# Row maxima of an attention kernel turned by a VectorE transpose of 32 by 32 blocks, in place of a matmul with the identity

## The chip, the cores and the metric

The kernel runs on one core of a Trainium2 chip. The metric is the device time of one execution in microseconds (us), smaller is better. A profile of one execution shows what each engine did: TensorE (PE, and PEld for its weight loads), VectorE (DVE), ScalarE (ACT), GpSimd (POOL) and SyncE (SP), whose queue issues most DMAs.

## The reference

One block of attention with 32 heads of 16 dimensions over 2048 rows, gated by a two-layer MLP of the same normalized input. All data are float32.

```python
xn = _layernorm(x, axis=-1)                                # x: 1 x 2048 x 512
qkv = (xn @ wqkv) ...                                      # 32 heads of 16
scores = jnp.einsum("bhqd,bhkd->bhqk", q, k) * (Dh ** -0.5)
p = _softmax(scores, axis=-1)
o = jnp.einsum("bhqk,bhkd->bhqd", p, v)
s = o.transpose(0, 2, 1, 3).reshape(B, S, D) @ wo
h = _gelu(jnp.einsum("bsd,df->bsf", xn, w1) + b1)          # F = 1376
g = _silu(jnp.einsum("bsf,fd->bsd", h, w2) + b2)
return x + s * g
```

## The kernel before

**Units.** The attention is cut into 32 units `u`: 8 groups of 4 heads times 4 chunks of 512 query rows. Every unit is worked twice. A first pass (`s_mm`, L179, and `s_max`, L185) makes the scores with the query rows on the partitions, one tile of 128 queries by 512 keys per head, and VectorE reduces each tile to maxima (`mx`). The tiles live in a ring of PSUM banks (`s_tile`): two banks in the first stage, three in the second. The second pass (`t_one`, L722 and L724) makes the scores again, this time with the keys on the partitions; two more rows of the contraction carry the negative maximum of each query, so that TensorE subtracts it, and ScalarE takes the exponential (`slot<-pst`, `slot<-ps`). `pv_step` (L787) multiplies by the values, with four heads in four column strips of 32, 16 steps per unit.

**The end of a unit.** When the first pass of a unit is done, its maxima must go from "query on the partition" to "query along the free axis". `s_end0` (L235) reduces the maxima of the key chunks on VectorE and negates them (`nm`, L240, 128 partitions by 4 heads x 4 query tiles), and POOL splits them into a rounded high part and the rest (`nmh`, L243 and L244: 128 x 2 x 16). Some 8 or 12 ticks later `s_end1` (L257) multiplies `nmh`, as weights, with the identity of 128 x 128 on TensorE. The result, 32 rows (part, head, query tile) of 128 queries, stands in a PSUM bank taken from the score ring (first stage) or from the ring of the second pass (`t_tile`, four banks). `s_end2` (L262) copies it to SBUF (`mh`), with ScalarE in the first stage (L265) and VectorE in the second (L267), and SP writes it to a scratch in DRAM (`mh_d`, L268). Later `load_mh` (L150) reads it back as the two more rows of `qt`.

**Stages.** From 57 us TensorE works at the MLP and the remaining projections (`mm`, L573), with two row halves of 64 rows used side by side, and `fill` interleaves 576 tiles of first-pass scores at due row counts. `FILL0`, `ROWS` and `put` set the due rows: an end takes a place in this order and moves what follows by two rows. From 484 us each of 512 steps holds four tiles of the second pass, the `pv` of the step before and three quarters of a score tile pair, in the order `TXSTTSTYV`; after the `V` the ticks advance and `flush` may end a unit. In the last part, from 1515 us, the first pass is over, and the steps hold output projections (`w_mul`, L79) in its place. The instruction order of every engine is written out by the program (a manual schedule); no planner decides it.

Of the kernel before, what the change touches and what calls it, by code (L numbers as in the profile page):

```python
# [8 lines left out]
F32 = mybir.dt.float32  # L9
F32R = mybir.dt.float32r  # L10
AF = mybir.ActivationFunctionType
# [5 lines left out]
P = 128  # L17
# [7 lines left out]
NCH = S // CH  # L25
F = 1376
FT = (F + P - 1) // P
GH = 4
# [4 lines left out]
LEAD = 144  # L33
# [3 lines left out]
FILL0 = 38  # L37
# [10 lines left out]
def fused(ctx: ExitStack, tc: tile.TileContext, x, wqk, wv, wo, w1, b1, w2, b2, out):  # L48
    nc = tc.nc
# [15 lines left out]
    mh_d = dpool.tile([NG * NCH, 2, GH, CH], F32, name="mh_d")  # L65

    ident_r = keep.tile([P, P], F32R, name="ident_r")
# [13 lines left out]
            if then:  # L81
                then()

    QS, QT, MX, NM, MH = {}, {}, {}, {}, {}
    SYNC = mybir.DependencyInfo(mybir.DependencyClass.Sync, mybir.DependencyReason.DATA)
    qss = []
    NU = NG * NCH
# [3 lines left out]
    def s_tile(held=False):  # L91
        pool = s_ring.pop(0)
        if not held:
            s_ring.append(pool)
        return pool.tile([P, CH], F32, name="ps"), pool
# [57 lines left out]
    made = [0, 0]  # L153
    done = {u: 0 for u in range(NU)}
    later, ended, errands, sent = [], [], [], set()

    def tick():
        for e in later:
            e[0] -= 1

    def flush():
        while later and later[0][0] <= 0:
            u = later.pop(0)[1]
            run_off()
            s_end1(u)
            s_end2(u)

    def at_of(job):
        u, st, p = job
# [29 lines left out]
    def s_one(a):  # L199
        made[a] += 1  # L200
        s_whole(heads[made[a] - 1], a)
# [29 lines left out]
    def run_off():  # L231
        while put_off:
            put_off.pop(0)()
# [21 lines left out]
    prog = {}  # L255

    def s_end1(u):  # L257
        pm = s_tile()[0] if "seen" in prog else t_tile()
        nc.tensor.matmul(pm[:2 * GH * NCH, :P], NM.pop(u).rearrange("p i a -> p (i a)"), ident_r, start=True, stop=True)  # L259
        MH[u] = pm  # L260

    def s_end2(u):  # L262
        mh = qring.tile([2 * GH * NCH, P], F32, name="mh", bufs=1)
        if "seen" in prog:
            nc.scalar.activation(mh, MH.pop(u)[:2 * GH * NCH, :P], AF.Copy)  # L265
        else:
            nc.vector.tensor_copy(mh, MH.pop(u)[:2 * GH * NCH, :P])  # L267
        nc.sync.dma_start(mh_d[u].rearrange("i j (q s) -> (i j q) s", s=P), mh)  # L268
        sent.add(u)

    sa = ExitStack()
# [19 lines left out]
    VQ = 3  # L291
    first = [[("v", t // NCH, t % NCH) for t in range(i, i + 4)] for i in range(NT - 4 * VQ, NT, 4)]
    qs = [(2, 0), (2, 2)] + [(g, 0) for g in range(3, NG)] + [(g, 2) for g in range(3, NG)]
    nu, pairs = len(ms) // 2, []
# [8 lines left out]
    for j in range(len(pairs)):  # L303
        for h in range(2):
# [4 lines left out]
            due = next((i for i in range(j, len(pairs)) if is_m[i]), len(pairs))  # L309
# [212 lines left out]
    qring = ctx.enter_context(tc.tile_pool(name="qring", bufs=2, side="right"))  # L522
# [16 lines left out]

    prog.update(n=0, pe=0, seen=0)  # L540
    writer = {}
    s_when, put, row = [], [0], [0, 0]
    ndown = sum(1 for e in plan if e[0] == "down")
    ROWS = 12 * (4 * VQ + 2 * len(pairs)) + 6 * ndown - 10 + 2 * LEAD - 2 * (LEAD // 16 - 1) - FILL0

    def fill(a):
        due = FILL0 + put[0] + sum(made) * ROWS // (4 * LEAD)
        if sum(made) < 4 * LEAD and row[a] >= due and (made[0] <= made[1]) == (a == 0):
            taken()
            if later and later[0][0] <= 0:  # L550
                put[0] += 2
                u = later.pop(0)[1]
                s_end1(u)
                s_end2(u)
                return
            s_one(a)
            row[a] += 1
            tick()

    def taken():  # L560
        prog["pe"] += 1
        s_when.append(prog["pe"])
        if len(s_when) > 2:
            prog["seen"] = max(prog["seen"], s_when[-3])
# [32 lines left out]
    def run(ops, hooks={}):  # L597
        for n, two in enumerate(zip(*ops)):
            prog["n"] += 1
            for a in range(2):  # L600
                fill(a)
                mm(a, *two[a])
            for h in hooks.get(n, []):
                h()
# [102 lines left out]
    def t_tile():  # L707
        turns[0] += 1
        if turns[0] < 5:
            pool = (ps_m, ps_x, ps_a, ps_b)[turns[0] - 1]  # L710
        else:
            pool = ps_m if turns[0] % 4 == 1 else ps_t
        return pool.tile([P, CH], F32, name="pst" if pool is ps_t else "ps")
# [230 lines left out]
    for n in range(L + 1):  # L944
        ua, ka = divmod(n, 16)
        want = due(n) - due(n - 1)
        i = 0
        for op in ORDER[want] if n > 1 else ("TTTTV", "TTSTSVT")[n]:
            if op in "SXY":
                s_op(op)  # L950
            elif op == "V":
                if n:
                    pv_step(*divmod(n - 1, 16))
                for _ in range(4):
                    tick()
                flush()
            else:
                if EARLY <= 4 * n + i < 4 * L:
                    t_one(ua, ka, i % 2, 1 - i // 2)
                for f, args in todo.get((n, i), []):  # L960
                    f(*args)
                i += 1
# [56 lines left out]
```

## Time and profile before

| | |
|---|---|
| median of 3 runs | 1606.27 us (1606.13 to 1606.79) |
| span of the profiled execution | 1603.9 us |
| PE busy | 1593.1 us, 99% |
| DVE busy | 1383.5 us, 86% |
| ACT busy | 1260.5 us, 79% |
| POOL busy | 377.5 us, 24% |

The profiled execution's own time is not listed apart from its span; the median of the runs lies 2.4 us above the span. A row of a group reads: line, engine, operation, what is written `<-` what is read, the form (partitions x elements, for matmuls rows*columns), the count, then busy us and the mean ns of one, then the idle time of the engine before them. A row of the order of time reads: start, length, engine, line, operation, and in brackets the idle time before it and what ended it. Ends of matmuls are modelled, so for TensorE the distance from start to start is what counts.

### The profile page before, as it was taken

How to read it: one execution, taken by the hardware profiler on the slowest of the kernel's cores; microseconds unless marked ns; L12 is line 12 of the kernel's file. 1: busy time of each engine (PE TensorE's matmuls, PEld its weight loads, DVE VectorE, ACT ScalarE, POOL GpSimd, SP SyncE). 2: the span in 40 equal slices, each digit the busy share in tenths (PEclk: the TensorE clock that was granted, in tenths of full speed). 3: DMA queues.
4: the chain of work that ended last, by engine and by line, in shares of the span. 5: the costliest groups of instructions: out<-in, count | busy, mean ns of one | idle time of the engine just before them, and what ended most of it. 6: DMA issues, size and time to landing. Idle time of an engine off the chain costs nothing.

```text
span 1603.9 us, 32476 instructions
## 1 busy us (share of the span) xinstructions
PE 1593.1 (99%) x12146; PEld 915.7 (57%) x12146; DVE 1383.5 (86%) x2267; ACT 1260.5 (79%) x2524; POOL 377.5 (24%) x398
## 2 busy tenths in 40 slices
PE   8999999999999999999999999999999999999998
PEld 7899989999994444444444444444444444444445
DVE  7489888888989999999999999999999999999734
ACT  4333443434339999999999999999999999999984
POOL 4145565766640001011100200100010000000144
PEclk9999999999999999999999999999999999999999
DMA  6525343454322113111410411221141111110152
GB/s 204 149 59 151 116 136 97 148 145 126 114 89 70 40 30 70 29 36 42 79 32 27 68 42 29 59 42 29 30 70 30 30 29 37 34 29 22 58 200 91
DMA packets 76798, 116.93 MB, mean 73 GB/s; under 512 B 25156, under 2 KB 26436, under 8 KB 75464
## 3 DMA queue, kind: packets, MB, share of 16 engines
q1 hardware_dynamic: 73180, 102.42, 22.4%
q0 software_dynamic: 3264, 12.35, 3.9%
q8 instruction: 96, 1.57, 0.4%
q14 instruction: 62, 0.51, 0.1%
q10 hardware_dynamic: 196, 0.07, 0.0%
HBM read 84.35 MB, written 25.97 MB: 69 GB/s over the span
## 4 chain that ended last, share of the span: by engine, by line
PE 97%; DVE 1%; ACT 0%; DMA 0%; issue 0%; SPq 0%; DVEq 0%; ACTq 0%
PE pv L787 32%; PE ps L179 18%; PE pst L722 16%; PE ps L573 12%; PE pst L573 7%; PE ps L722 5%; PE ps L79 3%; PE pv L573 2%; PE pst L79 1%; DVE slot L74 0%; DMA xt<-in_x 0%; PE pst L259 0%; DVE st L407 0%; PE ps L259 0%; DVE xn L421 0%
## 5 line engine op out<-in xcount | busy, mean ns | idle before, releaser
L185 DVE TENSOR_REDUCE mx<-ps 128x2 f32<-128x512 f32 x2048 | 1299.4, 685 | 153.3 <-PE ps L179 84.9
L724 ACT ACTIVATE slot<-pst 128x512 f32<-128x512 f32 x1533 | 835.1, 612 | 14.2 <-PE pst L722 4.1
L787 PE MATMUL pv<-slot,vsb 128*32 128x512 f32 x4096 | 545.3, 605 | 0.0
L179 PE MATMUL ps<-kt,slot 48*128 48x512 f32 (+1 forms) x1364 | 393.1, 376 | 0.0
L722 PE MATMUL pst<-qt,kt 50*128 50x512 f32 x1149 | 378.1, 430 | 0.5 <-DVE gt L655 0.3
L722 PEld LDWEIGHTS pst<-qt,kt 50*128 50x128 f32 x1149 | 183.0, 184 | 249.6 <-ACT slot L724 246.2
L724 ACT ACTIVATE slot<-ps 128x512 f32<-128x512 f32 x515 | 314.8, 612 | 12.9 <-PE pst L722 8.2
L179 PEld LDWEIGHTS ps<-kt,slot 48*128 48x128 f32 x1364 | 211.3, 184 | 34.2 <-DVE mx L185 23.3
L573 PE MATMUL ps<-slot,w1h 64*128 64x512 f32 x1088 | 220.5, 394 | 0.0
L179 PE MATMUL ps<-kt,qz 48*128 48x512 f32 x512 | 214.9, 420 | 0.0
L179 PE MATMUL ps<-slot,slot 48*128 48x512 f32 (+1 forms) x598 | 172.6, 376 | 0.0
L722 PE MATMUL ps<-qt,kt 50*128 50x512 f32 x387 | 163.0, 423 | 0.0
L573 PEld LDWEIGHTS ps<-slot,w1h 64*128 64x128 f32 x1088 | 152.9, 185 | 6.8 <-ACT junk L587 0.8
L787 PEld LDWEIGHTS pv<-slot,vsb 128*32 128x32 f32 x4096 | 80.6, 108 | 119.8 <-issue 112.0
L573 PE MATMUL ps<-slot,w1l 64*128 64x512 f32 x544 | 143.0, 392 | 0.0
L367 POOL TENSOR_TENSOR hl<-hg,hh 128x512 fp32r<-128x512 f32 x76 | 96.8, 1296 | 131.7 <-ACT hh L366 95.0
L722 PE MATMUL pst<-qt,slot 50*128 50x512 f32 x384 | 119.8, 424 | 0.0
L587 ACT ACTIVATE junk<-ident_r 1x1 f32<-1x1 f32 x92 | 18.0, 196 | 126.4 <-PE pst L573 123.2
L722 PEld LDWEIGHTS ps<-qt,kt 50*128 50x128 f32 x387 | 71.1, 184 | 69.4 <-ACT slot L724 56.5
L179 PEld LDWEIGHTS ps<-kt,qz 48*128 48x128 f32 x512 | 93.7, 183 | 17.4 <-DVE mx L185 0.6
L243 POOL CAST nmh<-nm 128x16 fp32r<-128x16 f32 x32 | 6.3, 197 | 413.1 <-PE pst L722 209.1
L722 PEld LDWEIGHTS pst<-qt,slot 50*128 50x128 f32 x384 | 61.5, 184 | 71.9 <-ACT slot L724 71.6
(150 smaller groups left out, 1744.9 us busy)
## 6 DMA issues: line engine op xcount, KB each, us to landing
raw<-in_w SPq DMA_DIRECT2D x88, 256.0 KB
qk_h<-hh SPq DMA_DIRECT2D x32, 256.0 KB
qk_l<-hl SPq DMA_DIRECT2D x32, 256.0 KB
qt<-qk_h SPq DMA_DIRECT2D x128, 64.0 KB
slot<-qk_h SPq DMA_DIRECT2D x92, 64.0 KB
xt<-in_x SPq DMA_DIRECT2D x16, 256.0 KB
g_d<-gt POOLq DMA_DIRECT2D x16, 256.0 KB, 3.1
qt<-qk_l SPq DMA_DIRECT2D x64, 64.0 KB
```

Source lines behind the costliest of these rows:

```text
L79: nc.tensor.matmul(ps, lhs[a], rhs[b], start=first and n == 0, stop=last and n == 2)
L179: return nc.tensor.matmul(ps[:, c0:c0 + w], QS[u][r, p, qi * P:(qi + 1) * P], kts[u // NCH % KB][p][r, k0:k0 + w], start=True, stop=True).ins
L185: nc.vector.tensor_reduce(MX[u][:, 2 * p:2 * p + 2, qi, ki][:, heads, parts], ps.rearrange("p (n c) -> p n c", c=HC), axis=AX.X, op=OP.max)
L243: nc.gpsimd.tensor_copy(hl[:, 0], nm)
L367: nc.gpsimd.tensor_sub(hl, raw, hh.bitcast(F32))
L573: i = nc.tensor.matmul(ps, lhs[r], rhs[r], start=first, stop=last).ins
L587: i = nc.scalar.activation(junk[:, :1], ident_r[:1, :1].bitcast(F32), AF.Copy).ins
L722: nc.tensor.matmul(ps, kts[g % KB][p][r, k * P:(k + 1) * P], QT[u][r, p, :], start=True, stop=True)
L724: nc.scalar.activation(PT[u, k][:, 2 * p + a, :], ps, AF.Exp, scale=SCALE)
L787: nc.tensor.matmul(PV[u][32 * j:32 * j + 32, :], vsb[:, k, h:h + 32], PT[u, k][:, j, :], start=(k == 0), stop=(k == NT - 1))
```

## The change

The matmul with the identity and the copy out of PSUM go. One VectorE instruction transposes the 128 x 32 elements of `nmh` in blocks of 32 by 32 within SBUF. Partition 32 b + r of `mh` then holds, for row r of (part, head, query tile), the 32 queries of block b. The DMA to `mh_d` puts this in order: 128 pieces of 32 elements, and not 32 pieces of 128. As an end no longer takes a place on TensorE, `put` and its part in `ROWS` go too, and `fill` puts a score tile in the same place.

```diff
     def s_end1(u):
-        pm = s_tile()[0] if "seen" in prog else t_tile()
-        nc.tensor.matmul(pm[:2 * GH * NCH, :P], NM.pop(u).rearrange("p i a -> p (i a)"), ident_r, start=True, stop=True)
-        MH[u] = pm
-
-    def s_end2(u):
-        mh = qring.tile([2 * GH * NCH, P], F32, name="mh", bufs=1)
-        if "seen" in prog:
-            nc.scalar.activation(mh, MH.pop(u)[:2 * GH * NCH, :P], AF.Copy)
-        else:
-            nc.vector.tensor_copy(mh, MH.pop(u)[:2 * GH * NCH, :P])
-        nc.sync.dma_start(mh_d[u].rearrange("i j (q s) -> (i j q) s", s=P), mh)
+        mh = qring.tile([P, 2 * GH * NCH], F32, name="mh", bufs=1)
+        nc.vector.transpose(mh, NM.pop(u).rearrange("p i a -> p (i a)").bitcast(F32))
+        nc.sync.dma_start(mh_d[u].rearrange("i j (q b s) -> b (i j q) s", b=NCH, s=2 * GH * NCH), mh)
         sent.add(u)
...
-    ROWS = 12 * (4 * VQ + 2 * len(pairs)) + 6 * ndown - 10 + 2 * LEAD - 2 * (LEAD // 16 - 1) - FILL0
+    ROWS = 12 * (4 * VQ + 2 * len(pairs)) + 6 * ndown - 10 + 2 * LEAD - FILL0
...
-        due = FILL0 + put[0] + sum(made) * ROWS // (4 * LEAD)
+        due = FILL0 + sum(made) * ROWS // (4 * LEAD)
...
             if later and later[0][0] <= 0:
-                put[0] += 2
-                u = later.pop(0)[1]
-                s_end1(u)
-                s_end2(u)
-                return
+                s_end1(later.pop(0)[1])
             s_one(a)
```

More of the change, by code (lines that the diff above doesn't have):

```diff
@@ L82, in mm3 @@
                 then()
-    QS, QT, MX, NM, MH = {}, {}, {}, {}, {}
+    QS, QT, MX, NM = {}, {}, {}, {}
     SYNC = mybir.DependencyInfo(mybir.DependencyClass.Sync, mybir.DependencyReason.DATA)
@@ L541, in fused @@
     writer = {}
-    s_when, put, row = [], [0], [0, 0]
+    s_when, row = [], [0, 0]
     ndown = sum(1 for e in plan if e[0] == "down")
-    ROWS = 12 * (4 * VQ + 2 * len(pairs)) + 6 * ndown - 10 + 2 * LEAD - 2 * (LEAD // 16 - 1) - FILL0
+    ROWS = 12 * (4 * VQ + 2 * len(pairs)) + 6 * ndown - 10 + 2 * LEAD - FILL0
     def fill(a):
-        due = FILL0 + put[0] + sum(made) * ROWS // (4 * LEAD)
+        due = FILL0 + sum(made) * ROWS // (4 * LEAD)
         if sum(made) < 4 * LEAD and row[a] >= due and (made[0] <= made[1]) == (a == 0):
@@ L550, in fill @@
             if later and later[0][0] <= 0:
-                put[0] += 2
-                u = later.pop(0)[1]
-                s_end1(u)
-                s_end2(u)
-                return
+                s_end1(later.pop(0)[1])
             s_one(a)
```

## The prediction

> **What bounds the kernel now.** I read the stretches first, to see which engine sets the pace of each stage; then the chain of waits, for what a unit of work takes with and without the step that changes; then the order of time around that step; then the groups of VectorE and the DMA issues. Rows of the stretches give start:end, length, and then for PE, PEld, DVE, ACT and POOL the busy time and the instructions.
>
> ```profile
> 57.00:484.00 427.00, 426.59 (x3545) 386.18 (x3545) 375.46 (x591) 163.35 (x369) 239.23 (x211) 1.00 0.41 119
> 484.00:1515.00 1031.00, 1030.89 (x7876) 441.44 (x7868) 939.52 (x1549) 1013.31 (x1994) 77.34 (x128) 1.00 0.18 41
> ```
>
> In the first stage (57 to 484) TensorE is never idle and ScalarE has much room. In the second (484 to 1515) TensorE is never idle either, ScalarE is busy for 98% and VectorE for 91%: whatever takes TensorE's time there costs its own length, and VectorE and ScalarE have little room to give. The granted clock is 1.00.
>
> What an end of a unit costs in the second stage is read from the chain of waits (start, length, what). These rows are the first `pv` matmul group of the units 1 to 5, each 16 steps after the one before.
>
> ```profile
> 519.96 1.06 PE pv L787 x8
> 553.70 1.06 PE pv L787 x8
> 587.46 1.07 PE pv L787 x8
> 620.83 1.06 PE pv L787 x8
> 654.36 1.06 PE pv L787 x8
> ```
>
> The stretch 587.46 to 620.83 takes 33.37 us and holds no end (no L259 matmul). The one from 620.83 takes 33.53 and holds one, at 623.84 below. The one from 519.96 takes 33.74 and holds one at 535.6. So an end costs 0.16 or 0.37, and the question is how much of the 0.37 is the matmul. In order of time on TensorE, and then on VectorE around 535.6:
>
> ```profile
> 623.84 0.25 PE L259 MATMUL pst<-ident_r,nmh 128*32 128x128 f32 x1
> 624.01 0.50 PE L722 MATMUL ps<-qt,kt 50*128 50x512 f32 x1
> ```
> ```profile
> 532.52 0.28 DVE L240 TENSOR_REDUCE nm<-mx 128x16 f32<-128x128 f32 x1
> 532.71 1.28 DVE L185 TENSOR_REDUCE mx<-ps 128x2 f32<-128x512 f32 x2
> 533.91 0.24 DVE L815 RECIPROCAL dr<-dr 128x16 f32<-128x16 f32 x1
> 534.07 1.84 DVE L185 TENSOR_REDUCE mx<-ps 128x2 f32<-128x512 f32 x3
> 535.87 0.28 DVE L267 COPY mh<-pst 32x128 f32<-32x128 f32 x1
> 536.42 0.69 DVE L185 TENSOR_REDUCE mx<-ps 128x2 f32<-128x512 f32 x1 [0.27 <-PE ps L179]
> ```
> ```profile
> 534.04 0.18 PEld L179 LDWEIGHTS ps<-slot,slot 48*128 48x128 f32 x1 [0.27 <-DVE mx L185]
> ```
>
> The next matmul starts 0.17 after L259, which is the whole 0.16. In the stretch with 0.37 there are also L240 and a reciprocal on VectorE, 1.5 to 3 us before the end, and behind them the weight load at 534.04 waits 0.27 for a `mx`: two short VectorE operations among the maxima held a PSUM bank of the score ring too long. That remains 0.21, and it stays: L240 and L815 are not touched.
>
> **The change part by part.** *Matmuls, stage two.* The groups of VectorE (line, operation, form, count | busy us, mean ns) give the number of ends.
>
> ```profile
> L240 DVE TENSOR_REDUCE nm<-mx 128x16 f32<-128x128 f32 x32 | 8.8, 276 | 0.1
> L815 DVE RECIPROCAL dr<-dr 128x16 f32<-128x16 f32 x32 | 7.8, 242 | 2.1 <-DMA dr<-os 2.1
> L267 DVE COPY mh<-pst 32x128 f32<-32x128 f32 x18 | 5.0, 276 | 0.1
> L267 DVE COPY mh<-ps 32x128 f32<-32x128 f32 x6 | 1.7, 277 | 0.1
> L848 DVE SCALAR_TENSOR_TENSOR slot<-slot,slot 128x512 f32<-128x512 f32 x4 | 7.3, 1825 | 0.4
> ```
>
> 32 ends, of which VectorE copies 24, so the other 8, copied by ScalarE, are in stage one. One of the 24 is in the tail (below). 23 x 0.16 = 3.7 us.
>
> *Matmuls, stage one.* Around an end there, on TensorE:
>
> ```profile
> 255.44 0.50 PE L573 MATMUL pst<-w2h,hh 64*128 64x512 f32 x2
> 255.88 0.25 PE L259 MATMUL ps<-ident_r,nmh 128*32 128x128 f32 x1
> 256.05 0.50 PE L573 MATMUL pst<-w2l,hh 64*128 64x512 f32 x2
> 256.39 0.40 PE L573 MATMUL pst<-w2h,hl 64*128 64x512 f32 x2
> 256.62 0.39 PE L179 MATMUL ps<-kt,qz 48*128 48x512 f32 x1
> 256.63 0.39 PE L573 MATMUL pst<-w2h,hh 64*128 64x512 f32 x1
> 256.86 0.39 PE L573 MATMUL pv<-w2h,hh 64*128 64x512 f32 x1
> 256.86 0.39 PE L573 MATMUL pst<-w2l,hh 64*128 64x512 f32 x1
> 257.09 0.39 PE L573 MATMUL pv<-w2l,hh 64*128 64x512 f32 x1
> ```
>
> From 256.62 to 257.09 four matmuls start, two at a time in the two row halves: 0.1175 each. From 255.44 to 256.62 six of them and L259 take 1.18; six alone would take 0.705. So L259, which uses all rows and lets nothing run beside it, costs 0.475 here, and 8 x 0.475 = 3.8 us. The slot that it held in the interleaving goes back to the scores: the due rows lose their 2 per end and the total gains the same 16, so the 576 score tiles of this stage still end with it.
>
> *The tail.* Steps start here at the output projection, from the chain of waits:
>
> ```profile
> 1515.47 1.60 PE ps L79 x6
> 1518.07 0.18 PE pst L259
> 1519.11 1.59 PE ps L79 x6
> 1522.36 1.59 PE ps L79 x6
> ```
>
> The step with the last end takes 3.64, the next 3.25. Of the 0.39 only 0.18 is L259; the rest lies in score matmuls that wait for banks, one of which L259 had taken. Between 0.18 and 0.39 I take 0.3.
>
> *The copies.* 8 on ScalarE in stage one: it is busy for 163 of 427 us, so nothing. 24 on VectorE, 0.276 each, give their place to the transpose.
>
> *The transpose*, 32 of them, 128 partitions by 32 elements. No row shows this operation. Nearest are L815 with 16 elements per partition (0.242) and L240 with 128 (0.276); the far end is L848 at 1.83, SBUF to SBUF too but 512 elements and two inputs. I take 0.26, the middle of the near pair. In stage two that is the copy's length, at the copy's place in VectorE's order. The copy's cover was partly L259 itself: without it the next maximum could start 0.17 sooner than 536.42, at 536.25, while a transpose begun at 535.87 ends at 536.13. So nothing is lost up to about 0.38; if the cover were gone, the price is what L240 and L815 cost, 0.21 per end. Below nothing: a gain is excluded where VectorE is not what TensorE waits for, but where an end falls beside an L240, up to the full 0.37 may go. In stage one the transposes are 8 x 0.26 = 2.1 us more for an engine that is busy for 375 of 427 us; hidden. A page of the Trainium skill, "VectorE: DVE Perf Modes", section "The three transpose paths", gives 311 ns for 128x128 of 2-byte elements on VectorE; by that price the sum would be the same, since it is under the 0.38. No run here shows it yet.
>
> *The new wait.* The transpose waits for POOL's `nmh`, as L259 did. Behind it in VectorE's order stand the score maxima, for which TensorE's score matmuls wait. POOL's second `nmh` operation, in stage two and in stage one:
>
> ```profile
> 534.35 0.22 POOL L244 TENSOR_TENSOR nmh<-nm,nmh 128x16 fp32r<-128x16 f32 x1
> ```
> ```profile
> 248.97 0.22 POOL L244 TENSOR_TENSOR nmh<-nm,nmh 128x16 fp32r<-128x16 f32 x1
> ```
>
> It is done 1.3 us before VectorE gets to 535.87, and 6.7 us before 255.88. In the built order two POOL subtractions stand ahead of `nmh` at three ends of stage one where they stood behind; even several us fit. No wait.
>
> *The write of the maxima.* Still one DMA per unit, of the same 16 KB, but from 128 partitions with 128 bytes each and not from 32 with 512. SP's queue (start, time to issue):
>
> ```profile
> 1518.59 0.32 SPq L268 DMA_DIRECT2D mh_d<-mh  x1
> 1521.68 1.36 SPq L150 DMA_DIRECT2D qt<-mh_d  x2
> 1538.66 0.32 SPq L816 DMA_DIRECT2D den_d<-dr  x1
> 1541.54 2.45 SPq L819 DMA_DIRECT2D dn<-den_d  x4
> ```
>
> L150 follows its write by 3.1 us. L816 writes 64 bytes from each of 128 partitions, issues in the same 0.32, and its reader follows after 2.9. So 128-byte lines need no more time: 0. Behind L268 and L150 in SP's queue stand loads and stores of other units, which then move by nothing either. What it costs if the row misleads is a rival below.
>
> *The sum:* 3.8 + 3.7 + 0.3 = 7.8 us. The profiled span of 1603.9 becomes 1596.1. The median of the runs, 1606.27, lies 2.4 above the span; that stays, so 1598.5.
>
> **The rivals.** *The transpose stalls as L240 does.* Among back-to-back maxima it holds a bank and TensorE loses 0.21 per end where it saved 0.16: stage two 23 x -0.05 = -1.2, in all 3.8 + 0.3 - 1.2 = 2.9, so 1603.4. For it: VectorE at 91%, and the wait at 534.04. Against: at the end's place VectorE idles 0.27 before the next maximum.
>
> *The whole 0.37 goes.* If L259 and the bank that it takes also make the wait at 534.04 dear, each end of stage two gives 0.37: 23 x 0.37 = 8.5, with 3.8 and 0.39 in all 12.7, so 1593.6. For it: the 33.74. Against: the wait comes before the matmul, and 33.53 shows ends without it.
>
> *The late write.* For the last unit the write and the read of the maxima stand 4 steps (of 3.25) ahead of the matmul that needs them: from about 1518.6 to 1528.1. If the read, whose issue ends at 1523.0, takes the 2.9 us that the write of L816 took, it lands at 1525.9, 2.2 ahead. If small lines doubled the write's 3.1, the matmul would wait 0.9: 1599.4. Against: L816. The Trainium skill, "DMA: Bandwidth & Descriptors", section "Specifications", states that below 512 B a transfer is done as a read-modify-write; that speaks against this change and would be the mechanism. The trace does not bear it out, since 64-byte lines took 2.9 and 512-byte lines 3.1.
>
> *Slower: the transpose is long.* If it took the 1.83 of L848, VectorE would come 1.83 - 0.38 = 1.45 late at each end of stage two, and with three banks always in use TensorE would lose that: 23 x 1.45 = 33. Stage one would lose at most the 8 x 1.83 = 15. Against the gain of 7.8 and with half of the latter, 1606.3 + 33 + 7 - 8 = 1638. It decides from a transpose of about 0.38 + 7.8 / 31 = 0.63 us. For it: no row of this operation. Against: all rows of short operands.
>
> **How the numbers follow.** Forecast 0.63, own range 1596 to 1601 (0.05 either way per end, stage one 3.0 to 4.1); a stall like L240's 0.13; all of it 0.11; late write 0.05; long transpose 0.08. 0.2% of the time, about what a measurement of this kernel can tell from no change, is 3.2 us, so faster means below 1603.1. Faster: 0.63 + 0.11 + 0.05 and 0.02 of the stall; same: 0.11 of it; slower: 0.08. The range goes from 1594.0 to 1603.5 and leaves out the long transpose and the edge of the two others.
>
> **What would show it.** Right: no L259; stretches between the `pv` rows at 33.35 to 33.6, with a short one near 33.4 also where an end lies; the first stage 3.8 shorter; a transpose row near 0.26; no idle time of DVE ascribed to L244; L150 about 3 us behind L268. Wrong: a transpose of over 0.4; weight loads of L179 that wait longer in total for `mx`; stretches still at 33.7; a wait for `qt` after 1515.

## The result, and the profile after

The changed kernel takes 1596.14 us (median; 1595.38 to 1596.83), the kernel before, on the same chip, 1606.53 (1606.13 to 1608.83). The ratio is 0.9937, with a 95% interval of 0.9925 to 0.995. The span of the profiled execution went from 1603.9 to 1593.6 us.

The stretches of the changed kernel, in the same columns as before (start:end, length, then busy time and instructions of PE, PEld, DVE, ACT and POOL):

```profile
57.00:480.00 423.00, 422.54 (x3544) 384.45 (x3545) 378.27 (x603) 162.97 (x364) 240.33 (x214) 1.00 0.42 122
480.00:1505.00 1025.00, 1024.99 (x7836) 439.12 (x7828) 935.20 (x1545) 1011.17 (x1991) 76.66 (x126) 1.00 0.19 41
```

TensorE still fills both stages, so what left its order left the time. The groups of VectorE by form (count | busy, mean ns | idle time before them):

```profile
L239 DVE TENSOR_REDUCE nm<-mx 128x16 f32<-128x128 f32 x32 | 8.8, 276 | 0.0
L802 DVE RECIPROCAL dr<-dr 128x16 f32<-128x16 f32 x32 | 7.8, 243 | 2.2 <-DMA dr<-os 2.2
L258 DVE STREAM_TRANSPOSE mh<-nmh 128x32 f32<-128x32 f32 x32 | 6.5, 202 | 0.0
```

The transpose takes 0.202 us, and the idle time ahead of all 32 of them is 0.0: none waits for POOL.

The chain of waits (start, length, what): the second `pv` group of the units 0 to 5, and the last steps with output projections around the last end. (The rows of the prediction, too, show each unit's second `pv` group and not its first; the unit lengths read from them are the same to some hundredths.)

```profile
479.71 1.07 PE pv L774 x8
...
513.09 1.06 PE pv L774 x8
...
546.62 1.07 PE pv L774 x8
...
580.21 1.06 PE pv L774 x8
...
613.60 1.07 PE pv L774 x8
...
646.96 1.07 PE pv L774 x8
...
1505.09 1.59 PE ps L79 x6
1508.34 1.60 PE ps L79 x6
1511.60 1.60 PE ps L79 x6
```

The units 0 to 4 now take 33.38, 33.53, 33.59, 33.39 and 33.36 us. Before there were 33.37 (no end), 33.53 and 33.74. The 33.74 became 33.53 to 33.59, and the 33.53 became 33.36 to 33.39, which is what a unit without an end takes. In the tail, steps take 3.25 and 3.26 where one took 3.64.

VectorE in order of time, around an end of the kind that cost 0.37 before:

```profile
527.02 0.24 DVE L802 RECIPROCAL dr<-dr 128x16 f32<-128x16 f32 x1
527.18 1.87 DVE L184 TENSOR_REDUCE mx<-ps 128x2 f32<-128x512 f32 x3
528.96 0.20 DVE L258 STREAM_TRANSPOSE mh<-nmh 128x32 f32<-128x32 f32 x1
529.35 1.89 DVE L184 TENSOR_REDUCE mx<-ps 128x2 f32<-128x512 f32 x3 [0.18 <-PE ps L178]
```

From the transpose to the next maximum there are 0.39 us. The transpose is done after 0.20, and VectorE idles for 0.18 until a score tile is there. Not every end has that much room. Here is an end in the stretch of unit 4, in which no `nm` stands; VectorE's idle time, 0.31, lies ahead of three maxima, and behind the transpose the next maximum follows after 0.21:

```profile
615.25 1.89 DVE L184 TENSOR_REDUCE mx<-ps 128x2 f32<-128x512 f32 x3 [0.31 <-PE ps L178]
617.05 0.20 DVE L258 STREAM_TRANSPOSE mh<-nmh 128x32 f32<-128x32 f32 x1
617.26 1.89 DVE L184 TENSOR_REDUCE mx<-ps 128x2 f32<-128x512 f32 x3
```

In the 30 units of the table below, the next maximum starts 0.38 to 0.45 after the transpose at the 15 ends whose stretch also holds an `nm`, 0.20 to 0.23 after it at 7 others, and 0.56 at the first. The last end in SP's queue:

```profile
1507.98 0.62 SPq L259 DMA_DIRECT2D mh_d<-mh  x1
1510.02 1.33 SPq L150 DMA_DIRECT2D qt<-mh_d  x2
```

The read follows its write by 2.04 us; before it was 3.1. The write takes 0.62 to issue where it took 0.32. But three reads of the maxima waited for their write in each kernel, and the last was the slow one of the kernel before. The waits of SP for that write (us in all, times, longest), before and after:

```profile
SPq L150 <- DMA mh_d<-mh: 5.2, 3, 2.7
```
```profile
SPq L150 <- DMA mh_d<-mh: 4.0, 3, 1.3
```

From write to read there were 1.95, 1.50 and 3.09 us before, and there are 2.04, 2.02 and 2.04 after.

To see where the time went, every execution is cut at the same marks. "Stage one" goes from the first to the last start of a matmul with 64 rows (L573 before, L560 after). "30 units" goes from the second `pv` group of unit 0 to that of unit 30, "last two" (units 30 and 31) from there to the start of the last `pv` group, and "end" from that start to the end of the span. The outer marks of stage one, before and after, in TensorE's order of time:

```profile
53.43 0.49 PE L573 MATMUL pst<-kt,slot 64*128 64x512 f32 x1
...
481.63 0.59 PE L573 MATMUL pst<-w2h,hl 64*128 64x512 f32 x2
```
```profile
52.35 0.50 PE L560 MATMUL pst<-kt,slot 64*128 64x512 f32 x1
...
474.99 0.58 PE L560 MATMUL pst<-w2h,hl 64*128 64x512 f32 x2
```

The second matmul of the last groups starts at 481.83 and 475.17. Table of marks, in us; the medians are of the experiments below:

```
                         start  stage one  30 units  last two  end    median   ratio, 95% interval
before                   53.43    428.40   1008.01    85.54   23.92  1606.53
after                    52.35    422.82   1004.31    85.20   24.38  1596.14  0.9937 [0.9925, 0.995]
order kept               53.10    424.55   1004.31    85.17   24.36  1597.95  0.9955 [0.994, 0.997]
matmul left              52.92    428.46   1008.43    85.37   23.94  1605.49  0.9999 [0.999, 1.0008]
stage one only           53.52    422.95   1008.40    85.57   23.94  1600.34  0.9966 [0.9953, 0.9979]
stage two only           52.91    428.47   1004.39    85.17   24.36  1602.22  0.9978 [0.9969, 0.9988]
four transposes          53.12    427.40   1011.09    85.16   24.36  1607.38  1.0013 [1.0003, 1.0022]
nm at flush              53.39    422.71   1001.29    85.13   24.35  1592.83  0.9923 [0.9908, 0.9937]
FILL0 36                 52.26    421.44   1004.04    85.18   24.36  1594.52  0.9932 [0.9917, 0.9947]
FILL0 40                 52.43    422.17   1003.97    85.17   24.37  1594.71  0.9935 [0.9918, 0.9952]
nm at flush, FILL0 36    53.08    421.48   1001.31    85.17   24.37  1591.80  0.9917 [0.99, 0.9933]
```

The 10.28 us that the span lost are 5.58 in stage one, 3.70 in the 30 units, 0.34 in the last two units and 1.08 at the start, less 0.46 at the end; the rest, 0.04, lies between stage one and the 30 units. The start varies between 52.26 and 53.52 among the profiles of these kernels, which are alike up to there. So the 1.08 is taken as chance in this pair of profiles, and as no gain of the change.

### The profile page after: what moved, and what is told of

Same layout as the page of the kernel before. It is cut to its first block, busy times and chain, and to the rows that moved or that the text cites. A ratio compares the mean times of both kernels' runs of the same rounds, so it can differ in the third digit from the quotient of the medians.

```text
span 1593.6 us, 32346 instructions
## 1 busy us (share of the span) xinstructions
PE 1583.3 (99%) x12114; PEld 911.8 (57%) x12114; DVE 1378.2 (86%) x2275; ACT 1257.6 (79%) x2516; POOL 379.3 (24%) x398
## 4 chain that ended last, share of the span: by engine, by line
PE 98%; DVE 1%; issue 0%; ACT 0%; DMA 0%; DVEq 0%; ACTq 0%
PE pv L774 32%; PE ps L178 18%; PE ps L560 12%; PE pst L709 11%; PE ps L709 10%; PE pst L560 7%; PE ps L79 4%; PE pv L560 2%; PE pst L79 1%; DVE slot L74 0%; DVE st L398 0%; DMA xt<-in_x 0%; DVE xn L412 0%; DVE slot L870 0%; PE pst L421 0%
## 5 line engine op out<-in xcount | busy, mean ns | idle before, releaser
L711 ACT ACTIVATE slot<-pst 128x512 f32<-128x512 f32 x1533 | 809.4, 617 | 0.8 <-PE pst L709 0.8
L709 PE MATMUL pst<-qt,kt 50*128 50x512 f32 x1149 | 303.7, 405 | 0.5 <-DVE gt L642 0.3
L560 PE MATMUL ps<-slot,w1h 64*128 64x512 f32 x1088 | 217.5, 394 | 0.0
L709 PE MATMUL ps<-qt,kt 50*128 50x512 f32 x387 | 190.9, 495 | 0.0
L560 PEld LDWEIGHTS ps<-slot,w1h 64*128 64x128 f32 x1088 | 149.9, 185 | 8.8 <-ACT junk L574 2.8
L560 PE MATMUL ps<-slot,w1l 64*128 64x512 f32 x544 | 140.7, 392 | 0.0
L178 PEld LDWEIGHTS ps<-slot,slot 48*128 48x128 f32 x598 | 92.6, 184 | 15.7 <-DVE mx L184 11.3
L709 PE MATMUL pst<-qt,slot 50*128 50x512 f32 x384 | 101.5, 405 | 0.0
```

Source lines behind the costliest of these rows:

```text
L178: return nc.tensor.matmul(ps[:, c0:c0 + w], QS[u][r, p, qi * P:(qi + 1) * P], kts[u // NCH % KB][p][r, k0:k0 + w], start=True, stop=True).ins
L560: i = nc.tensor.matmul(ps, lhs[r], rhs[r], start=first, stop=last).ins
L709: nc.tensor.matmul(ps, kts[g % KB][p][r, k * P:(k + 1) * P], QT[u][r, p, :], start=True, stop=True)
L711: nc.scalar.activation(PT[u, k][:, 2 * p + a, :], ps, AF.Exp, scale=SCALE)
```

## The experiments

The ratios are to the kernel before, which ran beside them (1605.78 beside the first four, 1605.41 beside the next four, 1605.21 beside the last).

**Due rows as before.** The matmul and the copy are gone, but an end again takes a place in `fill` and two due rows.

```diff
-    ROWS = 12 * (4 * VQ + 2 * len(pairs)) + 6 * ndown - 10 + 2 * LEAD - FILL0
+    ROWS = 12 * (4 * VQ + 2 * len(pairs)) + 6 * ndown - 10 + 2 * LEAD - 2 * (LEAD // 16 - 1) - FILL0
...
-        due = FILL0 + sum(made) * ROWS // (4 * LEAD)
+        due = FILL0 + put[0] + sum(made) * ROWS // (4 * LEAD)
...
+            if later and later[0][0] <= 0:
+                put[0] += 2
+                s_end1(later.pop(0)[1])
+                return
             taken()
-            if later and later[0][0] <= 0:
-                s_end1(later.pop(0)[1])
             s_one(a)
```

> The changed kernel, but an end still takes its place in the interleaving of the first stage and moves the due rows by two, so TensorE's order is that of the kernel before with the L259 matmuls left out. The kernel before took 1606.5, the changed one 1596.1; the first stage gained 5.6 us beside a start-up that was 1.1 shorter in the profile, where 3.8 were forecast. Theory A (the surplus of 1.8 comes from the shifted order of the score tiles): 1597.9, and the gain of the first stage falls back to 3.8. Theory B (the surplus comes from the matmul itself and the bank that it holds until ScalarE has copied it): 1596.1, first stage as in the changed kernel.

Measured: 1597.95 us. Stage one took 424.55, which is 3.85 less than before and 1.73 more than with the whole change; the 30 units took 1004.31, to the digit what they took with it. So the order of the score tiles is worth 1.73 us of stage one and nothing after it, and 3.85 is what the matmul itself took there. The transposes take nothing off it: behind each of the 8 of stage one VectorE idles for 0.08 to 0.24 us in this kernel.

**The matmul left in.** The transpose does the work, and the old matmul with the identity is issued ahead of it, into a bank of the same ring and in the old order (the edit of the due rows is not printed). Nothing copies or reads its result.

```diff
     def s_end1(u):
+        pm = s_tile()[0] if "seen" in prog else t_tile()
+        nc.tensor.matmul(pm[:2 * GH * NCH, :P], NM[u].rearrange("p i a -> p (i a)"), ident_r, start=True, stop=True)
         mh = qring.tile([P, 2 * GH * NCH], F32, name="mh", bufs=1)
```

> The transposes as in the changed kernel, and beside them the L259 matmuls and the order of the kernel before; nobody reads the result of the matmuls and no copy is made. Theory of the prediction (an end costs TensorE's own time, the copies are hidden): about 1606.5, everything is back, first stage 5.6 longer than in the changed kernel or 3.8 if the shifted order gave the rest. Theory B (a bank held until the copy is what costs the surplus): 1.8 less than the kernel before, 1604.7, since a bank that nobody reads is free at once.

Measured: 1605.49 us, and stage one at 428.46 and the 30 units at 1008.43 are back where they were before. TensorE's order of time in this kernel, around an end of stage two:

```profile
535.12 0.25 PE L258 MATMUL pst<-ident_r,nmh 128*32 128x128 f32 x1
535.29 0.50 PE L713 MATMUL pst<-qt,kt 50*128 50x512 f32 x1
```

The next matmul starts 0.17 later, as before. Without the copy no engine but TensorE has to do with this bank, and still the whole gain is gone. In stage one a cost of the transposes could in principle hide a gain from the missing copies. VectorE in order of time shows that it does not:

```profile
255.81 0.20 DVE L260 STREAM_TRANSPOSE mh<-nmh 128x32 f32<-128x32 f32 x1
256.60 0.69 DVE L184 TENSOR_REDUCE mx<-ps 128x2 f32<-128x512 f32 x1 [0.59 <-PE ps L178]
```

Behind each of the 8 transposes VectorE idles for 0.57 to 0.67 us. So the copies, and a bank that is held until its copy is done, cost nothing in the kernel before, and the transpose saves nothing on VectorE that would show: the gain is TensorE's time and the place in its order.

**The change in one stage only.** In the first kernel the matmul and the VectorE copy stand in the second stage and the tail, in the other the matmul and the ScalarE copy in the first, with the old order there. The edit of the first kernel, shortened:

```diff
+        if "seen" in prog:
             mh = qring.tile([P, 2 * GH * NCH], F32, name="mh", bufs=1)
             nc.vector.transpose(mh, NM.pop(u).rearrange("p i a -> p (i a)").bitcast(F32))
             nc.sync.dma_start(mh_d[u].rearrange("i j (q b s) -> b (i j q) s", b=NCH, s=2 * GH * NCH), mh)
+        else:
+            pm = t_tile()
+            nc.tensor.matmul(pm[:2 * GH * NCH, :P], NM.pop(u).rearrange("p i a -> p (i a)"), ident_r, start=True, stop=True)
...
```

> Transposes in the first stage, matmul and VectorE copy in the second and in the tail. If the gains of the stages add: the first stage is the changed kernel's, the second and the tail are the old ones, 3.7 + 0.3 = 4.0 slower than the changed kernel: 1600.1. If the second stage gains by something else than the 0.16 per end, its 30 units between the first pv groups do not return to 1008.0 us (changed kernel: 1004.3).

> Matmul, ScalarE copy and old order in the first stage, transposes in the second and in the tail. If the gains add: 1606.5 - 4.0 = 1602.5; the 30 units of the second stage take 1004.3 us as in the changed kernel, the first stage is the old one. If the first stage's 5.6 contains 1.8 that do not belong to it (start-up, chance): 1600.7.

Measured: 1600.34 with the change in stage one, 1602.22 with it in stage two and the tail. Stage one took 422.95 and 428.47, the 30 units 1008.40 and 1004.39. Each stage has its whole gain without the other: the shares of the time saved, 0.34% and 0.22%, add to 0.56%, where the whole change has 0.63% with an interval of 0.5 to 0.75%.

**Four transposes at each end.** Three more copies of the transpose, into a tile that nobody reads, lengthen the time for which VectorE is held.

```diff
         nc.vector.transpose(mh, nmt)
+        for _ in range(3):
+            nc.vector.transpose(qring.tile([P, 2 * GH * NCH], F32, name="mx4", bufs=1), nmt)
```

> The changed kernel with the transpose made four times at each end, three of them into a tile that nobody reads. In the changed kernel one took 0.20 us and the next maximum started 0.13 after it, so four hold VectorE for some 0.13 x 3 = 0.4 us more. The prediction's slack of 0.38 at an end of stage two is then used up by about 0.2: theory of the slack says that the 30 units of stage two take 1004.3 + 23 x 0.1 to 0.2 = 1006.6 to 1009, first stage unchanged at 422.8, in all 1598.5 to 1601. Rival (VectorE has no slack there, every 0.13 is paid by TensorE): 23 x 0.4 = 9 more in stage two and up to 3 in stage one: 1606 to 1608. Rival (VectorE never holds up TensorE at this place): 1596.1.

Measured: 1607.38 us, by 0.03 to 0.22% longer than the kernel before. VectorE in order of time, in this kernel, at an end of stage two and at one of stage one (the spare tile shows as `mx`):

```profile
534.38 0.20 DVE L259 STREAM_TRANSPOSE mh<-nmh 128x32 f32<-128x32 f32 x1
534.51 0.66 DVE L261 STREAM_TRANSPOSE mx<-nmh 128x32 f32<-128x32 f32 x3
535.09 2.52 DVE L184 TENSOR_REDUCE mx<-ps 128x2 f32<-128x512 f32 x4
```
```profile
255.77 0.20 DVE L259 STREAM_TRANSPOSE mh<-nmh 128x32 f32<-128x32 f32 x1
255.90 0.66 DVE L261 STREAM_TRANSPOSE mx<-nmh 128x32 f32<-128x32 f32 x3
256.48 1.93 DVE L184 TENSOR_REDUCE mx<-ps 128x2 f32<-128x512 f32 x3
```

Four transposes hold VectorE for 0.71 us, from the first start to the next maximum: the second starts 0.13 after the first, but the third and the fourth, which write the same spare tile, follow after 0.20 and 0.25, so the hold added, 0.58, was larger than the expected 0.4. In stage two the idle time ahead of the next maximum is gone. Of the 0.71, 0.39 was there to have at the end shown, so 0.32 per end should go; the 30 units lost 6.78 us at 23 ends, 0.295 each. That the mean comes out so well is in part luck, since the ends differ. Where there were 0.38 to 0.45, the unit became 0.25 longer on average (15 ends), where there were 0.20 to 0.23, it became 0.43 longer (7 ends), and at the first end, with 0.56, 0.06. The more room there was, the less was lost, and each loss is 0.05 to 0.09 under the 0.71 less the room. So the slack at the end of a step is real, but it is 0.2 us at some ends and 0.4 at others. One length of hold does not locate a break-even point.

In stage one there is no such slack in the new order. With one transpose, the next maximum there starts right behind it:

```profile
252.69 0.69 DVE L184 TENSOR_REDUCE mx<-ps 128x2 f32<-128x512 f32 x1 [0.15 <-PE pst L560]
253.29 0.20 DVE L258 STREAM_TRANSPOSE mh<-nmh 128x32 f32<-128x32 f32 x1
253.42 1.95 DVE L184 TENSOR_REDUCE mx<-ps 128x2 f32<-128x512 f32 x3
```

The hold there is 0.13 with one transpose and 0.71 with four. Stage one lost 4.58 us at 8 ends, 0.57 each: all of the 0.58 that was added. The waits of weight loads for a maximum in the first stage (us in all, times, longest), of the changed kernel and of this one:

```profile
PEld ps L178 <- DVE mx L184: 0.6, 4, 0.2
```
```profile
PEld ps L178 <- DVE mx L184: 5.7, 8, 0.7
```

They rise by 5.1 us, in 8 waits, one per end.

**The reduction to `nm` at the end of the step.** Some units with an end still took 33.53 to 33.59 in the changed kernel. The prediction put 0.21 of the former 0.37 down to `nm` and a reciprocal among the maxima. Here, in the second stage, the reduction is held until `flush`, at the end of a step.

```diff
-        nc.vector.tensor_reduce(nm, mx, axis=AX.X, op=OP.max, negate=True)
+        held = "seen" not in prog and u < NU - 1
+
+        def one():
+            nc.vector.tensor_reduce(nm, mx, axis=AX.X, op=OP.max, negate=True)
+            put_off.append(two)
...
-        put_off.append(two)
+        if held:
+            held_off.append(one)
+        else:
+            one()
...
     def flush():
+        while held_off:
+            held_off.pop(0)()
```

> In the second stage the reduction to nm is not put among the score maxima but at the end of the step, where the transpose stands too; all else as in the changed kernel. The prediction put 0.21 of the 0.37 of an end at 535.6 down to this operation; the units with such an end still take 33.57 in the changed kernel and the others 33.37. If that is right, the 15 units fall to about 33.4 and the kernel to 1596.1 - 15 x 0.2 = 1593.1. If the 0.2 belongs to the end itself (the transpose, the bank), the units stay at 33.57 and the time at 1596.1.

Measured: 1592.83 us. In the chain of waits of this kernel, the second `pv` groups of the units 0 to 5:

```profile
480.68 1.07 PE pv L785 x8
...
514.04 1.07 PE pv L785 x8
...
547.40 1.06 PE pv L785 x8
...
580.75 1.06 PE pv L785 x8
...
614.12 1.07 PE pv L785 x8
...
647.49 1.07 PE pv L785 x8
```

All five take 33.35 to 33.37 now, with an end or without. Of the 30 units one takes 33.55 and the others 33.34 to 33.41, and together they lost 3.02 us. VectorE in order of time shows where the reduction stands:

```profile
525.99 1.89 DVE L188 TENSOR_REDUCE mx<-ps 128x2 f32<-128x512 f32 x3
527.79 0.27 DVE L246 TENSOR_REDUCE nm<-mx 128x16 f32<-128x128 f32 x1
527.98 0.24 DVE L813 RECIPROCAL dr<-dr 128x16 f32<-128x16 f32 x1
528.14 1.86 DVE L188 TENSOR_REDUCE mx<-ps 128x2 f32<-128x512 f32 x3
529.92 0.20 DVE L269 STREAM_TRANSPOSE mh<-nmh 128x32 f32<-128x32 f32 x1
```

Together with the reciprocal it holds VectorE for 0.35, from 527.79 to 528.14. It costs nothing there, while in the midst of a step the reduction cost about 0.2. So it was its place among the maxima, not its length. The reciprocal, which stayed, had no part in it: the unit from 546.62 in the changed kernel took 33.59 although no reciprocal stands near its `nm`. And the place matters for what follows it: in units without an end the reduction stands at the same point of a step and costs nothing, and there VectorE idles for 0.31 soon behind it (615.25 above, with `nm` at 613.47).

**Another phase of the score tiles.** `FILL0` sets at which row the first score tile of stage one is due; one kernel has 36, as in the diff, the other 40.

```diff
-FILL0 = 38
+FILL0 = 36
```

> The changed kernel with all due rows of the score tiles of the first stage two earlier. Leaving out the place of an end gave 1.7 us beside the 3.85 of the matmul (first stage 424.55 with the places kept, 422.82 without). Theory A1 (the time depends on where the score tiles fall in the runs of twelve matmuls): the first stage changes by one or two us here too, either way: 421 to 425. Theory A2 (the hole of two rows at each of the 8 ends costs the 1.7): 422.8, and 1596.1 in all.

> As the run before with the due rows two later. Theory A1: 421 to 425, not the same as with 36 or 38. Theory A2: 422.8, and 1596.1 in all.

Measured: 1594.52 and 1594.71 us, stage one 421.44 and 422.17 against 422.82 with 38. Two due rows more or less at the start, with nothing else changed, move stage one by 0.65 to 1.38 us, where kernels with the same stage one differ by up to 0.24 in it (422.71 to 422.95). That is of the size of the 1.73 which the order of an end is worth, and speaks for the phase of the score tiles against the MLP's matmuls as its cause. Stage one is shorter with both new values than with 38, though, so these runs don't show that the 1.73 is a mere chance of the phase: a lasting gain from the two rows given back may be a part of it. How it divides stays open. The ratios of these two kernels to the one before are not told apart from that of the change by their intervals; the marks of the stages show the difference.

**Both favourable edits.** `nm` at the flush and `FILL0` at 36.

> Both of the favourable edits at once: the reduction to nm held until the point where flush ends a step, and FILL0 at 36. Theory (the second stage depends on nm's place alone, the first on the phase of the score tiles alone, and nothing passes from one to the other): first stage 421.4 us as with FILL0 36 alone, second stage's 30 units 1001.3 as with the reduction at flush alone, so about 1.4 below the reduction at flush alone: 1591.4 us, 0.991 of the kernel before. Rival (the stages are coupled, the later end of a stage shifts the phase of the next): one of the two lengths returns to that of the changed kernel, 422.8 or 1004.3, and the time lies at 1592.8 or above.

Measured: 1591.80 us (1591.66 to 1592.30), a ratio of 0.9917 [0.99, 0.9933], the shortest of all. Stage one 421.48 and the 30 units 1001.31 are the values of the two edits alone. The stages do not disturb each other.

## Why the prediction was right, and where it was off

1598.5 us was forecast, 1596.14 measured, inside the forecast's own range of 1596 to 1601, but by 0.14 us only; two of the four runs, 1595.38 and 1595.96, lie below it. The terms that the range names (0.05 at 23 ends, stage one up to 4.1) reach down to about 1597.0, so it is luck that the lower end was put at 1596. The span lost 10.28 where the sum had 7.8. Of the 2.48 between, 1.73 came from the order of the score tiles and 1.08 from the start, taken as chance; 0.46 went back at the end of the span, and the rest, 0.13, is made up of small differences in the other terms.

*Matmuls, stage two, 23 x 0.16 = 3.7.* Right: 3.70 in the 30 units, and all of it back with the matmul left in. The two kinds of ends both lost some 0.14 to 0.21. The 0.21 that "stays" did stay, and its cause was half right: of "two short VectorE operations among the maxima", only the reduction to `nm` costs it, and only where no idle time follows. The rival that the whole 0.37 goes fell, since the bank that L259 took costs nothing.

*Matmuls, stage one, 8 x 0.475 = 3.8.* Right: 3.85, with the order kept.

*The tail, 0.3.* Right: 0.34. But the end of the span became 0.46 longer, and that was in no term. It is 23.92 to 23.94 us with L259 in the second stage and the tail, and 24.35 to 24.38 in every kernel without it there. It is none of the kernel's own work: VectorE's last instruction ends 3.34 us before the end of the span before and 3.77 before it after. Of the three closing instructions of POOL named DRAIN (duration in ns, shortest/median/longest), the last takes 193 where it took 46, and starts 0.28 later:

```profile
L1015 POOLq DRAIN  x3: 46/107/6415, 1596.7 to 1603.6; - x3
```
```profile
L1002 POOLq DRAIN  x3: 107/193/6408, 1585.9 to 1593.2; - x3
```

Why it does so is open: no experiment was made on it.

*"The slot that it held in the interleaving goes back to the scores."* Here the prediction mis-sized a term: it counted that slot at 0, because the score tiles still end with the stage, and it measured 1.73 us. That is most of the 2.4 us by which the forecast was too high. The number of score tiles and rows did balance; that the distance of score tiles to the MLP's matmuls has a price of its own, 0.65 to 1.38 us for two rows at the start, was not looked for. The profile of before alone would not have given the size.

*The copies, 0.* Right: the kernel with the matmul and without the copy is no faster than the kernel before, and VectorE idles behind each transpose in it.

*The transpose, 0.26 between 0.242 and 0.276.* It took 0.202, less than both ends of the range: the form with 32 elements per partition is shorter than a reciprocal of 16. On the sum this has no effect, as it was "under the 0.38" either way. The slack itself is confirmed, but its size was read at one end, 535.87, and taken for all. It is 0.38 to 0.45 in the changed kernel at ends of that kind and 0.20 to 0.23 at 7 of the 23. The transpose fits into both. So the rivals of a stall and of a long transpose fell for the reason given, with less room than the prediction thought. The point from which the latter decides was put at 0.63 us, and a hold of 0.71 made the kernel 2.0 us slower than the one before (1607.38 against 1605.41). That agrees with the point, but it loses in another way: 4.58 us of it in stage one, where no slack was left. The Trainium skill's 311 ns for 128x128 of 2-byte elements ("VectorE: DVE Perf Modes", section "The three transpose paths") has no counterpart here, since this form has a quarter of the elements, at twice the width.

*The transposes of stage one, "hidden" beside an engine busy for 375 of 427 us.* This step was argued from a share of busy time, and that is not enough: four transposes cost their whole added hold there. With the order kept, one transpose per end is hidden, since VectorE idles behind each. In the changed order the next maximum follows at once, and whether the first transpose, 0.13 per end, is paid there, up to 1 us in 8 ends, was not separated from the gain.

*No wait for POOL, no late write.* Right: the idle time ahead of L258 is 0.0, and the read of the last unit follows its write by 2.04 us and not by more than 3.1. But that 3.1, on which the prediction rested, was the slowest of three: at the two other ends the distance became longer, from 1.95 and 1.50 to 2.04 and 2.02. The rule of the Trainium skill on transfers below 512 B ("DMA: Bandwidth & Descriptors", section "Specifications") is neither borne out nor ruled out by three pairs of which two became longer and one shorter. SP's issue of the write became longer, 0.62 against 0.32, which the prediction had taken from L816 as equal; no stage became longer for it.

*What would show it.* Of the signs named, one would have misled. Weight loads of the score matmuls that wait for `mx` were to tell "wrong" if they rose in all. Between 490 and 1500, of before, of the changed kernel and of that with `nm` at the flush (us in all, times, longest):

```profile
PEld ps L179 <- DVE mx L185: 33.5, 195, 0.3
```
```profile
PEld ps L178 <- DVE mx L184: 37.1, 213, 0.3
```
```profile
PEld ps L182 <- DVE mx L188: 29.0, 176, 0.2
```

They rose by 3.6 us with the change, while the same stage became 3.7 shorter. TensorE is busy for 1024.99 of the 1025.00 us from 480 to 1505 all the same, by the modelled ends of its matmuls, so these waits hardly stop it. The distances of the `pv` rows were the sign that held.

## What to carry to other kernels

Where TensorE is never idle, cost a matmul by the distance to the next start in its own neighbourhood: the same 128x32 matmul cost 0.17 us in a stream that uses all rows and 0.475 between matmuls that run two at a time in the row halves. The operation that replaces it on a nearly full engine is free as long as it fits the idle time ahead of that engine's next instruction at that place; this slack decides, not the share of busy time, and it has to be read at every kind of place: it was 0.2 us at some ends of the second stage, 0.4 at others, and nothing was left behind the transposes of the first stage in the new order. Work that must stand among back-to-back reductions belongs where that slack is: moving one reduction of 0.28 us by part of a step gave 3.0 us, nearly as much as the change gave in the same stage.

## What the runs showed of the hardware

The block transpose of 128 x 32 float32 takes 0.202 us as shown, but the next maximum, or a transpose into another tile, can start 0.13 after it, and transposes into one tile follow each other by 0.20 to 0.25: an instruction's length is not the time for which it holds its engine. With 128 pieces of 128 bytes in place of 32 pieces of 512, SP took 0.62 us to issue the write of the last end and not 0.32. The three reads that waited for such a write followed it by 2.02 to 2.04 us, where it had been 1.50, 1.95 and 3.09. And the matmul with the identity costs TensorE the same 0.17 whether its result is read or not.
